# Attention, soft mixture of experts and a wide layer on one core: the small passes of the first token group put in another order

## The chip, the core and the metric

The kernel runs on one core of a Trainium2 chip. A core has five engines that run at the same time and wait for each other by semaphores: TensorE (PE: matmuls, with its weight loads as PEld), VectorE (DVE), ScalarE (ACT), GpSimd (POOL) and SyncE (SP), which here only issues transfers. Each engine takes its instructions strictly in the order in which the program gives them. The metric is the device time of one execution in microseconds (us); lower is better.

## The reference, cut to what matters

Attention over 4 x 8 heads (576 positions, window of 32 positions) gives x of 2304 x 512; a soft mixture of 8 experts turns it into another x of 2304 x 512; the last layer is the one that the change is in:

```python
def _moe2_ref(x, w_in, w_out):            # x 2304x512, w_in 512x2048, w_out 2048x512
    h = x @ w_in
    g = h - np.tanh(h)
    return (g @ w_out).astype(np.float32)
```

The second x is c @ slot_out with c of 2304 x 32, so the kernel never forms it: it forms G = slot_out @ w_in (32 x 2048) and then h = c @ G. The weights w_in and w_out come as 64-bit floats.

## The kernel before, in words

**The last layer's loop** is in `second`. The 2048 hidden units are 16 blocks of 128 (f = 0 to 15), the 2304 tokens four groups of 6, 4, 4 and 4 tiles of 128 tokens. A step is one block for one group. Steps 0 to 7 are the first group (6 tiles, 768 tokens) with blocks 0 to 7; they are what the change is about, and the weights arrive and are prepared while these steps run. Later steps find them ready.

**One step i on TensorE** takes 18 matmuls of 512 columns (line 766): six times w_out's rounded half `whi` with the rounded half `ghi` of g, six times the rest `wlo` with `ghi`, six times `whi` with the rest `glo`. In the middle of the last six stand the two matmuls that make h of step i + 2 (`hidden`, line 735). In steps 0, 1, 2 and 4 there is a projection of w_in to G as well: `project_a` (line 708) between the first six and the next, `project_b` (line 715) after the fourth of the next. `project_a` writes into a free part of the PSUM tile that holds half of h of step i + 1, so it can't start before VectorE has read that half.

**The other engines, for step i + 1, during step i:** ScalarE squares h (line 737), VectorE makes g from it in two pairs of instructions, one pair for 256 columns and one for 512 (`cubic`, lines 744 and 745), ScalarE rounds it (`ghi`, line 751), GpSimd takes the rest (`glo`, line 756).

**Preparing a piece** of the weights (a piece is 128 columns of w_in, called i0 to i15, or 128 rows of w_out, o0 to o15) from its 64-bit form: a short pass makes the low 16 bits (the low pass, line 692 on ScalarE or 694 on GpSimd), a second short pass on GpSimd the top (line 696), and one on VectorE puts them together (`merge`, line 700). A piece of w_out is then rounded by ScalarE into `whi` (line 722), and GpSimd takes the rest `wlo` (line 723); these two are `split_out`. A piece of w_in goes to `project_a`, whose result ScalarE copies twice (lines 710 and 716) and VectorE completes (line 718) before the next `hidden` can use it.

**The order of the work** is written out by hand: the engines' orders follow the order of the calls in the loop over steps and two tables. `now[i]` names the pieces whose top pass (and, earlier, low pass) belongs to step i; `joins[i]` names the pieces merged in step i, first those merged after the rounding of g has been issued, then those merged at the end of the step. Twelve buffers hold 64-bit pieces; a merge frees one, and SyncE then issues the next load.

Of the kernel before, what the change touches and what calls it, by code (L numbers as in the profile page):

```python
# [71 lines left out]
def attention_moe_moe(ctx: ExitStack, tc: tile.TileContext, q, k, v, phi, w1, w2, w_in, w_out, cst, out, dbg=None):  # L72
# [537 lines left out]
    def words(t):  # L610
        r = t.bitcast(I32).rearrange("p (x two) -> p x two", two=2)
        return r[:, :, 1], r[:, :, 0]
# [9 lines left out]
    def second(raw, raws, cT, store):  # L622
# [53 lines left out]
        def drop(piece):  # L676
            raws.pop(piece)
            feed()


        def place(piece):
            kind, f = piece
            return more[:, 512 * (f % 3):512 * (f % 3 + 1)] if kind == "o" and f < NA else flat[:, 512 * (f % 8):512 * (f % 8 + 1)]
# [4 lines left out]
        def prep(piece, on_act=False, parts=(0, 1)):  # L688
            hi, lo = (raws[piece].bitcast(dt).rearrange("p (x four) -> p x four", four=4)[:, :, x] for dt, x in ((I16, 3), (U16, 1)))
            top, low = (place(piece).bitcast(dt).rearrange("p (x two) -> p x two", two=2)[:, :, x] for dt, x in ((BF16, 1), (I16, 0)))  # L690
            if 0 in parts and on_act:
                nc.scalar.activation(out=low, in_=lo, func=AF.Identity, scale=2.0 ** -13, bias=wround)
            elif 0 in parts:
                nc.gpsimd.tensor_scalar(out=low, in0=lo, scalar1=2.0 ** -13, scalar2=WROUND, op0=ALU.mult, op1=ALU.add)
            if 1 in parts:
                nc.gpsimd.tensor_scalar(out=top, in0=hi, scalar1=2.0, scalar2=-2.0, op0=ALU.min, op1=ALU.max)

        def merge(piece, keep=False):
            w = place(piece).bitcast(I32)
            nc.vector.scalar_tensor_tensor(out=w, in0=words(raws[piece])[0], scalar=3, in1=w, op0=ALU.logical_shift_left, op1=ALU.bitwise_xor)  # L700
            if not keep:
                drop(piece)
# [17 lines left out]
        def split_out(f):  # L720
            wf = place(("o", f))
            nc.scalar.copy(whi[:, f, :], wf)
            nc.gpsimd.tensor_tensor(out=wlo[:, f, :], in0=wf, in1=whi[:, f, :].bitcast(F32), op=ALU.subtract)
# [15 lines left out]
        def cubic(i):  # L739
            u, t = us.pop(i), el.tile([128, WMAX], F32, tag="t", name=f"t_{i}")  # L740
            ts[i] = t[:, 0:128 * steps[i][1]]
            for c, hp in hps[i]:
                hp = hp[:, 0:c.stop - c.start]
                nc.vector.scalar_tensor_tensor(out=hp, in0=hp, scalar=-2.0 / 15.0, in1=u[:, c], op0=ALU.mult, op1=ALU.mult)  # L744
                nc.vector.scalar_tensor_tensor(out=t[:, c], in0=u[:, c], scalar=-2.5, in1=hp, op0=ALU.add, op1=ALU.mult)  # L745
# [14 lines left out]
        def outer(i, t, acc, parts=(0, 1, 2)):  # L760
            t0, _, f = steps[i]
            ghi, glo = gg[i]
            whole = t0 == g3[0]
            for x in parts:
                g = (ghi, ghi, glo)[x][:, 128 * t:128 * (t + 1)]
                nc.tensor.matmul(acc, lhsT=g, rhs=(whi, wlo, whi)[x][:, f, :], start=x == 0 and f in ((0,) if whole else (0, NA)), stop=x == 2 and f in ((NF - 1,) if whole else (NA - 1, NF - 1)))  # L766
# [23 lines left out]
        pieces = lambda names: [(x[0], int(x[1:])) for x in names.split()]  # L790
# [2 lines left out]
        again = inner[:NA] + outers  # L793
        todo = pieces("i0 o0 i1 o1 i2 i3 o2 i4 i5 o3 o4 i6 i7 o5 o6 o7") + inner[NA:] + outers[NA:] + again
        now = {i: pieces(x) for i, x in enumerate(("o2 i4", "i5 o3", "o4 i6", "i7 o5", "o6", "o7"))}
        joins = {i: [pieces(y) for y in x] for i, x in enumerate((("i3", "o2"), ("i4", "i5 o3"), ("", "o4"), ("i6", "i7 o5"), ("", "o6"), ("", "o7")))}
        batch = {0: (2, 1), 1: (3, 1), 2: (4, 2), 4: (6, 2)}
        then = {NA + k + k // 2: x for k, x in enumerate(inner[NA:] + outers[NA:])}

# [47 lines left out]
        for i, (t0, n, f) in enumerate(steps):  # L847
            if f == 0 or f == NA and t0 != g3[0]:
                accs = [ps.tile([128, DM], F32, tag=f"acc{t}", name=f"acc{t}_{i}", bufs=1) for t in range(n)]
            first, last = i < NA, f in (NA - 1, NF - 1)  # L850
            if first and not last:
                p = batch.get(i)
                if i:
                    split_out(i + 1)
                for t in range(n):
                    outer(i, t, accs[t], (0,))
                cubic(i + 1)
                if i == 0:
                    split_out(1)
                    for piece in now[0]:  # L860
                        prep(piece, on_act=True, parts=(0,))
                for piece in now.get(i, ()):
                    prep(piece, parts=(1,))
                if p:
                    pj = hps[i + 1][0][1][:, 256:256 + 128 * p[1]]
                    project_a(*p, pj)
                for t in range(n):
                    outer(i, t, accs[t], (1,))
                    if p and t == 3:
                        project_b(*p, pj, (0,))  # L870
                split_g(i + 1, (0,))
                for piece in joins.get(i, ((), ()))[0]:
                    merge(piece)
                if p:
                    project_b(*p, pj, (1,))
                for t in range(n):
                    outer(i, t, accs[t], (2,))
                    if t == 2:
                        hidden(i + 2)
                for piece in now.get(i + 1, ()):  # L880
                    prep(piece, on_act=True, parts=(0,))
                split_g(i + 1, (1,))
                for piece in joins.get(i, ((), ()))[1]:
                    merge(piece)
            else:
                if first:
                    cubic(i + 1)
                if i + 1 < len(steps):
                    split_g(i + 1)
                if i == len(steps) - 2:  # L890
                    for t, j in ((0, 0), (1, 0), (0, 1), (1, 1), (2, 0), (2, 1), (3, 0), (3, 1)):
                        outer(i + j, t, accs[t])
                        if j:
                            finish(i + 1, t, accs[t])
                    break
                for x in (0, 1) if first else ():
                    for t in range(n):
                        outer(i, t, accs[t], (x,))
                if i + 2 < len(steps):
                    hidden(i + 2)  # L900
                    cubic(i + 2)
                for t in range(n):
                    outer(i, t, accs[t], (2,) if first else (0, 1, 2))
                    if last:
                        finish(i, t, accs[t])
                for piece in made:
                    split_out(piece[1])
                made = []
                for piece in ready:
                    merge(piece, keep=piece[0] == "i")  # L910
                    if piece[0] == "i":
                        check.append(piece)
                    else:
                        made.append(piece)
                ready = [then[i]] if i in then else []
                for piece in ready:
                    prep(piece, on_act=True)
                for k, at in enumerate((NA, NA + 4)):
                    at += NA - 2 + 2 * k
                    if i in (at, at + 1):  # L920
                        (project_a, project_b)[i - at](NA + 4 * k, 4, ps.tile([128, 512], F32, tag="acc5", name=f"g{i - at}_{k}", bufs=1))
                if i == NB0:
                    assert not check
                    check = list(again)
                for _ in range(min(len(check), 1)):
                    inspect(check.pop(0))
                if NA <= i < 2 * NA or NB0 <= i < NB0 + NA:
                    nc.vector.tensor_reduce(out=gmx[:, f if i >= NB0 else i - NA:][:, 0:1], in_=Gs[:, 128 * (f if i >= NB0 else i - NA):][:, 0:128].bitcast(F32), axis=AX.X, op=ALU.max, apply_absolute_value=True)
                if i == len(steps) - NA:
                    assert not check and not todo  # L930
                    judge()
                if i == len(steps) - NA + 2:
                    verdict()
            gg.pop(i)
            hps.pop(i, None)
# [167 lines left out]
```

## Time and profile before

| | |
|---|---|
| time, median of 3 runs | 442.32 us (441.25 to 442.57) |
| the profiled execution | 443.09 us, its span 441.3 us |
| TensorE | busy 414.5 us, 94% of the span |
| VectorE | busy 314.8 us, 71% |
| ScalarE | busy 235.2 us, 53% |
| GpSimd | busy 209.5 us, 47% |
| mean granted clock of TensorE | 0.978 of full speed |

The span is the time from the first to the last instruction of that one execution; the time of an execution is 1.8 us longer. A share of busy time is a mean over stages, so it says which engine leads, and not where it waits: for that one goes to the waits of the engine in a stretch and to the order of its instructions in time.

### The profile page before, as it was taken

What the parts mean: (1) busy time and instruction counts of PE and PEld (TensorE: products, weight loads), DVE (VectorE), ACT (ScalarE), POOL (GpSimd) and SP (SyncE); (2) the same over time, 40 slices, a digit from 0 to 9 for tenths busy, and PEclk for the clock granted to TensorE, in tenths of its full rate; (3) what the DMA queues carried; (4) which work ended last, traced back from release to release, by engine and by line L of the source; (5) the groups of instructions that cost most, each with busy time, mean ns of one, the idle gap of its engine ahead of it and who ended that gap; (6) DMA issues with size and microseconds to landing.
All of it is one profiled execution on the core that took longest, in us unless ns stands there. A gap on an engine that the chain in (4) does not pass through costs nothing.

```text
span 441.3 us, 8666 instructions
## 1 busy us (share of the span) xinstructions
PE 414.5 (94%) x3000; PEld 316.9 (72%) x3000; DVE 314.8 (71%) x879; ACT 235.2 (53%) x503; POOL 209.5 (47%) x230
## 2 busy tenths in 40 slices
PE   8989969999998999999779999999999999999994
PEld 5879858878875644356558776777888788888773
DVE  5787856887876362248766678877879987799852
ACT  2565654657854232158645567666775745456430
POOL 1663534543520011069765555458993443434340
PEclk9998987999999999999988999999999999999999
DMA  5698997889897889999751122333445552030202
GB/s 152 168 242 228 222 244 192 228 243 253 254 312 269 335 298 408 401 369 381 250 187 53 42 97 95 97 99 110 128 142 190 195 188 97 0 143 1 95 0 102
DMA packets 59585, 82.84 MB, mean 188 GB/s; under 512 B 22928, under 2 KB 45072, under 8 KB 59536
## 3 DMA queue, kind: packets, MB, share of 16 engines
q1 hardware_dynamic: 59536, 82.23, 58.5%
q8 instruction: 25, 0.41, 0.4%
q14 instruction: 24, 0.20, 0.2%
HBM read 77.50 MB, written 4.72 MB: 186 GB/s over the span
## 4 chain that ended last, share of the span: by engine, by line


## 5 line engine op out<-in xcount | busy, mean ns | idle before, releaser
L756 POOL TENSOR_TENSOR glo<-t,ghi 128x512 fp32r<-128x512 f32 (+2 forms) x63 | 92.5, 1469 | 88.6 <-ACT ghi L751 86.2
L766 PE MATMUL acc<-whi,glo 128*128 128x512 f32 x288 | 108.5, 396 | 0.5 <-POOL glo L756 0.4
L766 PE MATMUL acc<-wlo,ghi 128*128 128x512 f32 x288 | 108.8, 399 | 0.0
L766 PE MATMUL acc<-whi,ghi 128*128 128x512 f32 x288 | 107.5, 395 | 0.2 <-ACT ghi L841 0.2
L751 ACT CAST ghi<-t 128x512 fp32r<-128x512 f32 (+1 forms) x63 | 42.4, 673 | 72.0 <-PE acc L766 33.3
L744 DVE SCALAR_TENSOR_TENSOR h<-h,u 128x512 f32<-128x512 f32 (+1 forms) x78 | 50.2, 644 | 28.9 <-ACT u L737 27.7
L766 PEld LDWEIGHTS acc<-whi,glo 128*128 128x128 f32 x288 | 54.5, 189 | 14.8 <-POOL glo L756 2.4
L766 PEld LDWEIGHTS acc<-wlo,ghi 128*128 128x128 f32 x288 | 54.4, 191 | 13.4 <-issue 1.2
L766 PEld LDWEIGHTS acc<-whi,ghi 128*128 128x128 f32 x288 | 53.9, 188 | 12.7 <-ACT ghi L841 0.8
L745 DVE SCALAR_TENSOR_TENSOR t<-u,h 128x512 f32<-128x512 f32 (+1 forms) x78 | 49.7, 637 | 6.9 <-POOL glo L756 0.5
L737 ACT ACTIVATE u<-h 128x512 f32<-128x512 f32 (+1 forms) x78 | 41.5, 552 | 4.6 <-PE h L735 4.6
L302 ACT COPY pT<-pp 96x512 f32<-96x512 f32 x38 | 22.2, 583 | 34.4 <-PE pp L301 33.9
L283 DVE CUSTOM_DVE_ANT_0 sm<-sc,m_sb 128x96 f32<-128x96 f32 x144 | 29.4, 259 | 14.9 <-PE sc L279 10.7
L279 PE MATMUL sc<-kT,qbd 128*128 128x96 f32 x272 | 39.7, 287 | 0.3 <-DVE kT L210 0.2
L279 PEld LDWEIGHTS sc<-kT,qbd 128*128 128x128 f32 x272 | 35.1, 199 | 2.8 <-issue 1.8
L154 POOL TENSOR_SCALAR km<-k 72x512 f32<-72x512 f32 x30 | 20.4, 695 | 25.7 <-DMA k<-in_k 12.6
L154 POOL TENSOR_SCALAR qm<-q 72x512 f32<-72x512 f32 x30 | 19.1, 652 | 27.7 <-DMA q<-in_q 14.0
L312 PE MATMUL pv<-vw,pT 96*64 96x65 f32 x608 | 26.7, 228 | 3.8 <-POOL vw L177 3.7
L735 PE MATMUL h<-cT,Gs 128*128 128x512 f32 (+1 forms) x78 | 29.0, 398 | 0.3 <-DVE t L745 0.2
L312 PEld LDWEIGHTS pv<-vw,pT 96*64 96x64 f32 x608 | 21.1, 137 | 10.1 <-issue 4.2
L301 PE MATMUL pp<-c_sb,sm 128*96 128x128 f32 x152 | 23.9, 281 | 0.7 <-ACT sm L294 0.7
L287 DVE TENSOR_TENSOR sm<-sm,mx 128x384 f32<-128x384 f32 (+1 forms) x38 | 22.3, 588 | 1.2
(193 smaller groups left out, 674.8 us busy)
## 6 DMA issues: line engine op xcount, KB each, us to landing
w<-in_moe_w SPq DMA_DIRECT2D x60, 512.0 KB
raw_o<-in_moe_w_out SPq DMA_DIRECT2D x32, 512.0 KB
raw_i<-in_moe_w_in SPq DMA_DIRECT2D x22, 512.0 KB
q<-in_q SPq DMA_DIRECT2D x32, 144.0 KB
k<-in_k SPq DMA_DIRECT2D x32, 144.0 KB
out<-X SPq DMA_DIRECT2D x17, 256.0 KB
vw<-in_v SPq DMA_DIRECT2D x16, 144.0 KB
vw<-in_v SPq DMA_DIRECT2D x32, 64.0 KB
```

The lines of the kernel that those rows point to most:

```text
L154: nc.gpsimd.tensor_scalar(out=dst, in0=src, scalar1=1.0, scalar2=0.0, op0=ALU.mult, op1=ALU.add)
L279: nc.tensor.matmul(sc[:, o:o + n, :].rearrange("p g k -> p (g k)"), lhsT=qbd[u % NQ][:, j].rearrange("p a n -> p (a n)"), rhs=keys, start= ...
L283: nc.vector.tensor_tensor_reduce(out=sm[:, o:o + n, :].rearrange("p g k -> p (g k)"), in0=sc[:, o:o + n, :].rearrange("p g k -> p (g k)"), ...
L301: nc.tensor.transpose(pp[:, i, :], sm[:, i, :], ident)
L312: nc.tensor.matmul(pv[64 * ab:64 * ab + 64, i, :], lhsT=pT[:, o + x, 64 * ab:64 * ab + 64], rhs=w[:, ab, u % 2, j + x, :], start=x == 0, s ...
L735: nc.tensor.matmul(hp[:, 0:y - x], lhsT=Gs[:, 128 * f:128 * (f + 1)], rhs=cT[:, t0 + x:t0 + y], start=True, stop=True)
L737: nc.scalar.activation(out=us[i][:, c], in_=hp[:, 0:c.stop - c.start], func=AF.Square)
L744: nc.vector.scalar_tensor_tensor(out=hp, in0=hp, scalar=-2.0 / 15.0, in1=u[:, c], op0=ALU.mult, op1=ALU.mult)
L745: nc.vector.scalar_tensor_tensor(out=t[:, c], in0=u[:, c], scalar=-2.5, in1=hp, op0=ALU.add, op1=ALU.mult)
L751: nc.scalar.copy(gg[i][0], ts[i])
L756: nc.gpsimd.tensor_tensor(out=glo[:, 0:p], in0=t[:, 0:p], in1=ghi[:, 0:p].bitcast(F32), op=ALU.subtract)
L766: nc.tensor.matmul(acc, lhsT=g, rhs=(whi, wlo, whi)[x][:, f, :], start=x == 0 and f in ((0,) if whole else (0, NA)), stop=x == 2 and f in ...
```

## The change

In the first group's steps the merges of the pieces move. Before, most of them stand at a step's end, ahead of the next step's `cubic` on VectorE; now they stand in the middle of the next step, behind its `cubic`. The rounding of the next piece of w_out (`split_out`) moves from a step's beginning to the place behind that merge. The low passes of w_out's pieces move by a step, and the low passes of i5 and i7 go from ScalarE to GpSimd, where the short passes of a step now stand ahead of that step's rounding rest.

```diff
-        joins = {i: [pieces(y) for y in x] for i, x in enumerate((("i3", "o2"), ("i4", "i5 o3"), ("", "o4"), ("i6", "i7 o5"), ("", "o6"), ("", "o7")))}
+        joins = {i: [pieces(y) for y in x] for i, x in enumerate((("i3", ""), ("o2 i4", "i5"), ("o3", ""), ("o4 i6", "i7"), ("o5", ""), ("o6", ""), ("o7", "")))}
+        both = pieces("i5 i7")
+        aside = {i: pieces(x) for i, x in enumerate(("o2 i4", "o3", "o4 i6", "o5", "o6", "o7"))}
...
-                if i:
-                    split_out(i + 1)
                 for t in range(n):
                     outer(i, t, accs[t], (0,))
                 cubic(i + 1)
                 if i == 0:
                     split_out(1)
-                    for piece in now[0]:
-                        prep(piece, on_act=True, parts=(0,))
                 for piece in now.get(i, ()):
-                    prep(piece, parts=(1,))
+                    prep(piece, parts=(0, 1) if piece in both else (1,))
...
                 for piece in joins.get(i, ((), ()))[0]:
                     merge(piece)
+                if i:
+                    split_out(i + 1)
                 if p:
                     project_b(*p, pj, (1,))
...
-                for piece in now.get(i + 1, ()):
+                for piece in aside.get(i, ()):
                     prep(piece, on_act=True, parts=(0,))
```

On VectorE, from the merge of i4 in step 1 on. Here `raw_i_48`, `raw_i_47`, `raw_o_46`, `raw_o_45`, `raw_i_44`, `raw_i_43`, `raw_o_42` are the 64-bit forms of i4, i5, o3, o4, i6, i7, o5 (the number counts the loads still to come), and L744 and L745 are the `cubic` of step 3. Before:

```order
L700 SCALAR_TENSOR_TENSOR X_79<-raw_i_48_2846,X_79 128x512
L718 TENSOR_TENSOR Gs<-h_2_3082,Gs 64x128
L700 SCALAR_TENSOR_TENSOR X_79<-raw_i_47_2848,X_79 128x512
L700 SCALAR_TENSOR_TENSOR more<-raw_o_46_2850,more 128x512
L744 SCALAR_TENSOR_TENSOR h_3_3137<-h_3_3137,u_3136 128x256
L745 SCALAR_TENSOR_TENSOR t_3163<-u_3136,h_3_3137 128x256
L744 SCALAR_TENSOR_TENSOR h_3139<-h_3139,u_3136 128x512
L745 SCALAR_TENSOR_TENSOR t_3163<-u_3136,h_3139 128x512
L718 TENSOR_TENSOR Gs<-h_3_3137,Gs 64x256
```

and now:

```order
L700 SCALAR_TENSOR_TENSOR X_79<-raw_i_48_2846,X_79 128x512
L718 TENSOR_TENSOR Gs<-h_2_3080,Gs 64x128
L700 SCALAR_TENSOR_TENSOR X_79<-raw_i_47_2848,X_79 128x512
L744 SCALAR_TENSOR_TENSOR h_3_3136<-h_3_3136,u_3135 128x256
L745 SCALAR_TENSOR_TENSOR t_3156<-u_3135,h_3_3136 128x256
L744 SCALAR_TENSOR_TENSOR h_3138<-h_3138,u_3135 128x512
L745 SCALAR_TENSOR_TENSOR t_3156<-u_3135,h_3138 128x512
L700 SCALAR_TENSOR_TENSOR more<-raw_o_46_2850,more 128x512
L718 TENSOR_TENSOR Gs<-h_3_3136,Gs 64x256
```

The merge of o3 has gone behind the `cubic` of step 3; i5's stays ahead of it.

On VectorE again, from step 3's `cubic` (which makes g of step 4) to that of step 4. Before:

```order
L744 SCALAR_TENSOR_TENSOR h_3194<-h_3194,u_3191 128x512
L745 SCALAR_TENSOR_TENSOR t_3215<-u_3191,h_3194 128x512
L700 SCALAR_TENSOR_TENSOR X_79<-raw_i_44_2854,X_79 128x512
L700 SCALAR_TENSOR_TENSOR X_79<-raw_i_43_2893,X_79 128x512
L700 SCALAR_TENSOR_TENSOR more<-raw_o_42_2898,more 128x512
L744 SCALAR_TENSOR_TENSOR h_5_3238<-h_5_3238,u_3237 128x256
L745 SCALAR_TENSOR_TENSOR t_3263<-u_3237,h_5_3238 128x256
```

and now:

```order
L744 SCALAR_TENSOR_TENSOR h_3192<-h_3192,u_3189 128x512
L745 SCALAR_TENSOR_TENSOR t_3208<-u_3189,h_3192 128x512
L700 SCALAR_TENSOR_TENSOR more<-raw_o_45_2852,more 128x512
L700 SCALAR_TENSOR_TENSOR X_79<-raw_i_44_2854,X_79 128x512
L700 SCALAR_TENSOR_TENSOR X_79<-raw_i_43_2893,X_79 128x512
L744 SCALAR_TENSOR_TENSOR h_5_3237<-h_5_3237,u_3236 128x256
L745 SCALAR_TENSOR_TENSOR t_3257<-u_3236,h_5_3237 128x256
```

There are three merges between the two in either order; o5's has left the place, o4's has come to it.

On GpSimd, from the rest `glo` of step 3 to that of step 4, before:

```order
L756 TENSOR_TENSOR glo_3185<-t_3163,ghi_3184 128x768
L723 TENSOR_TENSOR wlo<-more,whi 128x512
L696 TENSOR_SCALAR X_79<-raw_i_43_2893 128x512
L696 TENSOR_SCALAR more<-raw_o_42_2898 128x512
L756 TENSOR_TENSOR glo_3229<-t_3215,ghi_3228 128x768
```

and now:

```order
L756 TENSOR_TENSOR glo_3178<-t_3156,ghi_3177 128x768
L694 TENSOR_SCALAR X_79<-raw_i_43_2893 128x512
L696 TENSOR_SCALAR X_79<-raw_i_43_2893 128x512
L696 TENSOR_SCALAR more<-raw_o_42_2898 128x512
L723 TENSOR_TENSOR wlo<-more,whi 128x512
L756 TENSOR_TENSOR glo_3223<-t_3208,ghi_3222 128x768
```

i7's low pass (line 694) is new here, and w_out's rest (line 723) stands behind the short passes, next to `glo`.

## Rows read from the trace of the kernel before

**Rows 1.** The page, part 1: busy time, share of the span, instructions.

```profile
PE 414.5 (94%) x3000; PEld 316.9 (72%) x3000; DVE 314.8 (71%) x879; ACT 235.2 (53%) x503; POOL 209.5 (47%) x230
```

**Rows 2.** Waits, 199 to 249.2 us: who waited for whom: us, times, longest.

```profile
PE h L708 <- DVE t L745: 5.2, 2, 2.8
```

**Rows 3.** Waits of TensorE, 245 to 441 us.

```profile
PE acc L766 <- POOL glo L756: 0.4, 1, 0.4
PE h L735 <- DVE t L745: 0.2, 1, 0.2
```

**Rows 4.** TensorE in time: start, us, instruction, count, [idle before, releaser].

```profile
211.47 1.55 PE L766 MATMUL acc<-whi,ghi 128*128 128x512 f32 x6
215.45 0.64 PE L708 MATMUL h<-X,soT 128*32 128x256 f32 x8 [2.42 <-DVE t L745]
...
218.64 0.56 PE L735 MATMUL h<-cT,Gs 128*128 128x256 f32 x2
...
219.73 1.55 PE L766 MATMUL acc<-whi,ghi 128*128 128x512 f32 x6
221.12 1.53 PE L766 MATMUL acc<-wlo,ghi 128*128 128x512 f32 x6
...
224.20 1.53 PE L766 MATMUL acc<-whi,ghi 128*128 128x512 f32 x6
228.50 1.08 PE L708 MATMUL h<-X,soT 128*32 128x256 f32 x8 [2.77 <-DVE t L745]
...
235.49 1.53 PE L766 MATMUL acc<-whi,ghi 128*128 128x512 f32 x6
...
239.94 1.53 PE L766 MATMUL acc<-whi,ghi 128*128 128x512 f32 x6
```

**Rows 5.** Stretches: length, busy PE, PEld, DVE, ACT, POOL, granted clock, DMA share, GB/s.

```profile
224.20:228.50 4.30, 1.53 (x7) 0.96 (x6) 4.27 (x5) 1.54 (x3) 3.02 (x3) 0.91 0.68 226
...
230.00:232.00 2.00, 2.00 (x7) 1.53 (x6) 0.00 (x0) 0.01 (x1) 0.31 (x1) 0.50 0.09 37
```

**Rows 6.** VectorE in time, columns as in rows 4.

```profile
210.99 1.15 DVE L700 SCALAR_TENSOR_TENSOR X<-raw_i,X 128x512 int32<-128x512 int32 x1 [0.93 <-POOL X L696]
212.07 2.32 DVE L700 SCALAR_TENSOR_TENSOR more<-raw_o,more 128x512 int32<-128x512 int32 x1
214.42 0.43 DVE L744 SCALAR_TENSOR_TENSOR h<-h,u 128x256 f32<-128x256 f32 x1
...
215.95 0.69 DVE L745 SCALAR_TENSOR_TENSOR t<-u,h 128x512 f32<-128x512 f32 x1
...
225.26 2.30 DVE L700 SCALAR_TENSOR_TENSOR more<-raw_o,more 128x512 int32<-128x512 int32 x1
227.49 0.42 DVE L744 SCALAR_TENSOR_TENSOR h<-h,u 128x256 f32<-128x256 f32 x1
```

**Rows 7.** GpSimd in time, columns as in rows 4.

```profile
205.65 2.27 POOL L756 TENSOR_TENSOR glo<-t,ghi 128x768 fp32r<-128x768 f32 x1
...
211.59 2.24 POOL L756 TENSOR_TENSOR glo<-t,ghi 128x768 fp32r<-128x768 f32 x1
215.17 1.30 POOL L723 TENSOR_TENSOR wlo<-more,whi 128x512 fp32r<-128x512 f32 x1 [1.33 <-ACT whi L722]
...
224.08 0.78 POOL L696 TENSOR_SCALAR more<-raw_o 128x512 bf16<-128x512 int16 x1
224.79 2.22 POOL L756 TENSOR_TENSOR glo<-t,ghi 128x768 fp32r<-128x768 f32 x1
...
238.91 1.84 POOL L756 TENSOR_TENSOR glo<-t,ghi 128x768 fp32r<-128x768 f32 x1
```

**Rows 8.** ScalarE in time, columns as in rows 4.

```profile
217.95 0.84 ACT L751 CAST ghi<-t 128x768 fp32r<-128x768 f32 x1
219.00 0.87 ACT L737 ACTIVATE u<-h 128x256 f32<-128x256 f32 x2 [0.21 <-PE h L735]
...
221.22 0.62 ACT L722 CAST whi<-more 128x512 fp32r<-128x512 f32 x1
```

## The prediction, as it was put on record

> **What bounds the kernel now.** I read the page's busy shares first: TensorE leads with 94% [rows 1], so a microsecond is only won where TensorE waits or runs slow. Then its waits. From 245 us on it waits 0.6 us in all until the end [rows 3], so nothing is to be had there and whatever is won before goes through to the end. In the first group one pair stands out: `project_a` (line 708) waits twice for VectorE's `cubic` (line 745), 5.2 us together [rows 2]. TensorE's rows in time show where: at 215.45 in step 2 and at 228.50 in step 4 [rows 4].
>
> What each costs comes from the steps themselves. Steps 2 and 4 have the same instructions. Six matmuls are issued in 1.39 us (219.73 to 221.12), and from `project_a` to the next step's first matmul step 2 takes 4.28 us (215.45 to 219.73), so the step without a wait is 5.67 us [rows 4]. Step 2 took 8.26 us (211.47 to 219.73): 2.59 us too long, all of it the gap. Step 4 took 11.29 us (224.20 to 235.49): 5.62 us too long [rows 4], of which 2.91 us are the gap (228.50 less 224.20 and 1.39) and 2.71 us a slower clock: the same work after `project_a` took 6.99 us and not 4.28. Around this gap the granted clock fell to 0.91 of full speed on average and then stood at 0.50, the lower level of 1.2 GHz [rows 5]; after the gap of step 2 it did not fall, since the same work there needed no more than 4.28 us. Together 8.21 us.
>
> Why `cubic` is late is seen by laying VectorE's rows beside GpSimd's. The merge of o3 takes 2.32 us, from 212.07 to 214.39, while GpSimd's `glo` runs to 213.83; in step 4 o5's takes 2.30 us, to 227.56, with `glo` to 227.01 [rows 6, 7]. Both end 0.56 us behind GpSimd's end, so a merge waits until the GpSimd instruction beside it is over and then needs 0.56 us. `cubic`, queued behind it, starts at 214.42 and 227.49, and its first pair is what `project_a` waits for [rows 6]. A merge gets its turn between two GpSimd instructions: i5's ran 1.15 us to 212.14, and `glo`, next in GpSimd's order from 211.59, was stretched to 2.24 us where it takes 1.84 otherwise [rows 6, 7].
>
> **The change part by part.** TensorE's instructions and order stay as they are, and so do VectorE's count and the loads' order. I lay the steps out by hand with these durations: merge 0.56 us behind GpSimd's end; short pass 0.71 us back to back (224.08 to 224.79), `wlo` 1.30, `glo` 1.84 [rows 7]; first pair of `cubic` 0.85 us (two of 0.43), all four 2.22 us (214.42 to 216.64) [rows 6]; `ghi` 0.84, both squares 0.87, the first after 0.4, `whi` 0.62 [rows 8]; `hidden` 3.19 us behind `project_a` (218.64) [rows 4].
>
> *Step 2.* The merge of o3 leaves the place ahead of `cubic`. i5's stays. On GpSimd three short passes now follow the `glo` of step 1, which ended at 207.92 stretched [rows 7] and should end near 207.6: with a turn for the merges of o2 and i4 between them they end near 210.85 (207.6 + 3 x 0.71 + 2 x 0.56), and i5's merge near 211.4. ScalarE's first square is there by then too (`hidden` stands 1.09 us ahead of a step's first matmul, 218.64 to 219.73 [rows 4], so at 210.4), and `cubic` runs from 211.45. Its first pair is done at 212.3, and TensorE wants it at 212.86 (211.47 + 1.39). The gap of 2.59 us goes; step 3 starts near 217.1 instead of 219.73.
>
> *What is late next, step 4.* `wlo` of o2 now goes ahead of `glo` on GpSimd: 211.4 to 212.7, then `glo` to 214.5. The merge of o3, behind `cubic` (to 213.7), waits for that and ends at 215.05. `whi` of o3, now behind `ghi` of step 3 on ScalarE, ends at 216.75; the squares for step 4 queue behind it, so that `cubic` in step 3 runs from 217.2 to 219.4. On GpSimd `wlo` goes from 216.8 to 218.1 and `glo` to 219.95. Now merges and short passes take turns: merge o4 to 220.5, i7's low pass to 221.2, merge i6 to 221.75, i7's top pass to 222.45, o5's pass to 223.15, merge i7 to 223.7. Only then does step 4's `cubic` start; its first pair ends at 224.55 and `project_a` starts at 224.65. Step 4 begins at 217.13 plus 4.47 (step 3 has no wait: 219.73 to 224.20 [rows 4]), 221.6, and wants `project_a` at 223.0. So a gap of 1.65 us stays of the 2.91. Is it long enough for the clock? The gap of 2.59 us in step 2 was not [rows 4], so I take the full clock and win the 2.71 us too.
>
> *Costs put at little.* The low passes of i5 and i7 add two GpSimd instructions, 1.4 us; they are in the chain above, and i5's runs ahead of step 2 beside TensorE's step 1. On ScalarE the low passes only move to idle time. Loads: by this hand schedule the passes of i4, i5, o3 and i6 come later than before, so their loads have more time; the next group wants its pieces 6 us sooner, but SyncE issues those loads on the merges, which shift with the steps. `whi` on ScalarE is due at a step's start: o3's at 216.75 for 217.1, o4's at 221.2 for 221.6, so it holds, with 0.4 us to spare. `glo` is due after twelve matmuls, 2.8 us into a step without projection: 219.95 against 219.9 in step 3. From there a loop runs through the steps: end of `glo`, merge 0.56, `whi` 0.62, `wlo` 1.30, `glo` 1.84, and three hand-overs of some 0.05: 4.47 us. A step of TensorE is 4.45 us (235.49 to 239.94 [rows 4]). The two are equal, so `glo` comes just in time or a little late in steps 3, 5 and 6; I take 0.3 us for all of them, between 0 and 1.5 (0.3 in each of five steps).
>
> **The sum.** 8.21 less 1.65 less 0.3 is 6.3 us won. Against the profiled execution's 443.09 us this is 436.8; the median of the runs lies 0.77 us lower, so 442.32 becomes 436.0 us. Ends of the unknowns: if merges and passes meet less often (the chain without o5's pass and one wait, 1.3 us) almost no gap stays in step 4, 434.4, and no more than 8.21 can be won, 434.1. If the `glo` loop takes its 1.5, 437.2.
>
> The rule that speaks most against this change is in the Trainium skill, SBUF — State Buffer, section Who interferes with whom: VectorE with two inputs in SBUF and GpSimd exclude each other for the whole instruction, and the order of issue decides who waits. The trace agrees as far as [rows 6, 7] show it, and they add that the turn changes after each instruction. Read without that turn, the merges of o2 and i4 in step 1 would wait for two short passes more, 1.4 us; the instruction behind them (line 718) holds up `hidden`, step 2 would start that much later, and the sum would come to 437.4.
>
> **The rivals.**
>
> *A, the clock falls all the same.* The gap that stays in step 4 is followed by the slow level as before: 2.71 us more, 438.7. For it: the clock did fall at this place, behind a gap only 0.3 us longer than that of step 2. Against it: the gap of 2.59 us in step 2 left the clock as it was, and 1.65 us is well below it. It would take some 1 us more in the chain to step 4.
>
> *B, GpSimd becomes the bound.* The loop of 4.47 us has one short pass in the way in each of steps 3 to 7, 0.78 us each: five times that, 3.9 us, gives 439.9. For it: the loop has no slack, and the page's 47% of GpSimd hides that it is nearly full in these steps. Against it: the short pass stands where GpSimd waits for `whi` anyway (merge, hand-over and `whi` take 1.2 us, the pass behind the merge 1.3).
>
> *C, slower.* The same loop, but each merge meets a whole `glo` more: 1.84 us, 6.3 us a step against 4.45. Over steps 3 to 7 that is 9.2 us and eats the 8.21, so 443.3, and 446.0 with one fall of the clock. It decides from a loop of 6.1 us on. Against it: the merge stands directly behind one `glo`, and the next `glo` needs that merge's own `whi` through `wlo`'s place in the order, so a merge can't meet two.
>
> *D, nothing stays.* The time is given back in the later groups, because GpSimd or a load is late there: 442.3. Against it: TensorE waits 0.6 us there in all [rows 3], and those steps depend on this group's end only through TensorE's own order.
>
> **How the numbers follow.** The forecast (434.1 to 437.4) has 0.68, A 0.14, B 0.08, D 0.06, C 0.04. The range of 434.0 to 439.2 holds the forecast and most of A. A measurement of this kernel can tell 0.3%, 1.3 us, from no change. Forecast, A and B are faster by more than that, 0.90; D is the same, 0.06; C slower, 0.04.
>
> **What would show it.** Right: `project_a` in step 2 without a wait; in step 4 a gap of 1 to 2 us behind `cubic`; no stretch at 0.50 of the clock after 200 us; merges of w_out's pieces of 0.7 to 1.2 us behind `cubic`, each ending 0.56 us behind a `glo`; step 6 starting near 233.6 instead of 239.94. Wrong: TensorE waiting for `glo` or `whi` in each of steps 3 to 7 (B, C), a stretch at half clock (A), or new waits behind 243 us (D).

## The result, and the profile after

The changed kernel takes 436.83 us (median of 4 runs, 436.69 to 437.73) against 442.44 us of the kernel before beside it (4 runs, 441.25 to 444.16): a ratio of 0.9874 with an interval of 0.9839 to 0.991. Forecast were 436.0 us and a range of 434.0 to 439.2. Ratios and intervals, here and below, are taken over the faster executions alone, so they need not be the quotient of the medians beside them. The profiled execution took 436.85 us with a span of 435.1 us, where the one of before had 443.09 and 441.3.

The page's first part after the change:

```profile
PE 412.4 (95%) x3000; PEld 315.1 (72%) x3000; DVE 314.3 (72%) x879; ACT 233.8 (54%) x501; POOL 210.9 (48%) x232
```

The busy shares hardly moved [rows 1]; the waits did. First those of TensorE from 199 to 245 us, then those from 240 to 436 us (the pair, us in all, times, longest):

```profile
PE h L708 <- DVE t L745: 1.0, 1, 1.0
...
PE acc L766 <- POOL glo L756: 0.4, 1, 0.4
PE acc L766 <- ACT ghi L751: 0.2, 1, 0.2
PE h L735 <- DVE t L745: 0.2, 1, 0.2
```

`project_a` waits once and for 1.0 us where it waited twice and for 5.2 [rows 2], and behind the group TensorE waits 0.8 us in all where it waited 0.6 [rows 3]. TensorE in time after the change:

```profile
200.02 1.35 PE L766 MATMUL acc<-whi,ghi 128*128 128x512 f32 x4
...
211.62 1.55 PE L766 MATMUL acc<-whi,ghi 128*128 128x512 f32 x6
213.11 0.64 PE L708 MATMUL h<-X,soT 128*32 128x256 f32 x8
...
217.40 1.54 PE L766 MATMUL acc<-whi,ghi 128*128 128x512 f32 x6
...
220.24 0.96 PE L766 MATMUL acc<-whi,glo 128*128 128x512 f32 x3
...
222.09 1.55 PE L766 MATMUL acc<-whi,ghi 128*128 128x512 f32 x6
224.63 0.64 PE L708 MATMUL h<-X,soT 128*32 128x256 f32 x8 [1.00 <-DVE t L745]
...
228.91 1.55 PE L766 MATMUL acc<-whi,ghi 128*128 128x512 f32 x6
...
233.58 1.52 PE L766 MATMUL acc<-whi,ghi 128*128 128x512 f32 x6
...
242.53 0.39 PE L766 MATMUL acc<-whi,ghi 128*128 128x512 f32 x1
```

What the whole group took is read from the first matmul of step 0 to that of step 8. Before, these two stood at:

```profile
199.89 1.34 PE L766 MATMUL acc<-whi,ghi 128*128 128x512 f32 x4
...
249.12 0.39 PE L766 MATMUL acc<-whi,ghi 128*128 128x512 f32 x1
```

The start of a step is read off its first row of `whi` with `ghi`. Step 2 takes 5.78 us (211.62 to 217.40) instead of 8.26, step 4 takes 6.82 (222.09 to 228.91) instead of 11.29 [rows 4]. Steps 3 and 5 take 4.69 and 4.67, some 0.2 more than before: the three matmuls that first need `glo` start 2.84 us into step 3 (220.24) instead of 2.75, and take 0.96 us instead of 0.84. From step 0 to step 8 the group takes 42.51 us (it starts at 200.02) instead of 49.23 (199.89 to 249.12): 6.72 us less. Of these the span kept 6.2. The same stretches as in [rows 5]:

```profile
224.20:228.50 4.30, 3.87 (x23) 2.84 (x24) 3.37 (x5) 2.01 (x5) 3.62 (x3) 1.00 0.74 244
230.00:232.00 2.00, 2.00 (x9) 1.41 (x9) 1.97 (x3) 0.86 (x2) 2.00 (x2) 1.00 0.00 0
```

The granted clock is 1.00 in both, the upper level of 2.4 GHz. VectorE in time after the change:

```profile
211.31 0.43 DVE L744 SCALAR_TENSOR_TENSOR h<-h,u 128x256 f32<-128x256 f32 x1
...
213.45 1.27 DVE L700 SCALAR_TENSOR_TENSOR more<-raw_o,more 128x512 int32<-128x512 int32 x1
...
219.51 1.23 DVE L700 SCALAR_TENSOR_TENSOR more<-raw_o,more 128x512 int32<-128x512 int32 x1
220.65 1.20 DVE L700 SCALAR_TENSOR_TENSOR X<-raw_i,X 128x512 int32<-128x512 int32 x1
222.53 1.16 DVE L700 SCALAR_TENSOR_TENSOR X<-raw_i,X 128x512 int32<-128x512 int32 x1 [0.68 <-POOL X L696]
223.61 0.42 DVE L744 SCALAR_TENSOR_TENSOR h<-h,u 128x256 f32<-128x256 f32 x1
```

and GpSimd:

```profile
212.34 1.83 POOL L756 TENSOR_TENSOR glo<-t,ghi 128x768 fp32r<-128x768 f32 x1
...
218.31 1.87 POOL L756 TENSOR_TENSOR glo<-t,ghi 128x768 fp32r<-128x768 f32 x1
220.27 1.11 POOL L694 TENSOR_SCALAR X<-raw_i 128x512 int16<-128x512 uint16 x1
221.44 1.05 POOL L696 TENSOR_SCALAR X<-raw_i 128x512 bf16<-128x512 int16 x1
222.43 0.78 POOL L696 TENSOR_SCALAR more<-raw_o 128x512 bf16<-128x512 int16 x1
223.14 1.69 POOL L723 TENSOR_TENSOR wlo<-more,whi 128x512 fp32r<-128x512 f32 x1
```

Step 2's `cubic` starts at 211.31, 0.31 us ahead of the step; before it was 2.95 us behind the step's start. The merges of o3 and o4 end at 214.72 and 220.74, 0.55 and 0.56 us behind a `glo` (214.17 and 220.18); they take 1.27 and 1.23 us, a little more than the 0.7 to 1.2 that the prediction gave as a sign. In step 3 one sees the turns: merge of o4, i7's low pass (stretched to 1.11 us), merge of i6, i7's top pass (1.05), o5's pass, merge of i7, then `cubic` at 223.61. Between the merge of i6 and that of i7 VectorE is idle for 0.68 us, since i7's top pass isn't done.

### The profile page after: what moved, and what is told of

Its sections match the earlier page's. It is cut to its first block, busy times and chain, and to the rows that moved or that the text cites. A ratio compares the mean times of both kernels' runs of the same rounds, so it can differ in the third digit from the quotient of the medians.

```text
span 435.1 us, 8667 instructions
## 1 busy us (share of the span) xinstructions
PE 412.4 (95%) x3000; PEld 315.1 (72%) x3000; DVE 314.3 (72%) x879; ACT 233.8 (54%) x501; POOL 210.9 (48%) x232
## 4 chain that ended last, share of the span: by engine, by line
## 5 line engine op out<-in xcount | busy, mean ns | idle before, releaser
L756 POOL TENSOR_TENSOR glo<-t,ghi 128x512 fp32r<-128x512 f32 (+2 forms) x63 | 91.0, 1445 | 82.8 <-ACT ghi L751 79.0
L766 PE MATMUL acc<-wlo,ghi 128*128 128x512 f32 x288 | 107.4, 393 | 0.0
L744 DVE SCALAR_TENSOR_TENSOR h<-h,u 128x512 f32<-128x512 f32 (+1 forms) x78 | 50.3, 645 | 32.3 <-ACT u L737 31.1
L745 DVE SCALAR_TENSOR_TENSOR t<-u,h 128x512 f32<-128x512 f32 (+1 forms) x78 | 49.7, 637 | 7.6 <-POOL glo L756 0.5
L154 POOL TENSOR_SCALAR km<-k 72x512 f32<-72x512 f32 x30 | 19.4, 661 | 26.2 <-PE pp L301 8.4
L287 DVE TENSOR_TENSOR sm<-sm,mx 128x384 f32<-128x384 f32 (+1 forms) x38 | 23.8, 626 | 1.2
```

Of the source, the lines that this page charges most:

```text
L154: nc.gpsimd.tensor_scalar(out=dst, in0=src, scalar1=1.0, scalar2=0.0, op0=ALU.mult, op1=ALU.add)
L756: nc.gpsimd.tensor_tensor(out=glo[:, 0:p], in0=t[:, 0:p], in1=ghi[:, 0:p].bitcast(F32), op=ALU.subtract)
```

## The experiments

A gap below is, as in the prediction, the start of `project_a` less the step's start and 1.39 us; "behind it" is the time from `project_a` to the next step's first matmul, 4.28 us at the full clock. The halves, the halved `glo` and the low passes on ScalarE ran on one chip, where the kernel before took 443.32 us (25 runs, 439.59 to 448.28); the filled gaps, o5's pass, the change once more and the last version ran on another, where it took 442.55 (28 runs, 437.52 to 446.58). Three more profiles of the kernel before come from a third chip. Each experiment has one profile.

### One half of the change at a time

The early half has steps 0 to 2 as in the change and the rest as before, the late half the steps from 3 on. The edits against the change, early half:

```diff
-joins = ... ("o3", ""), ("o4 i6", "i7"), ("o5", ""), ("o6", ""), ("o7", "")
+joins = ... ("o3", "o4"), ("i6", "i7 o5"), ("", "o6"), ("", "o7")
...
-                if i:
+                if 0 < i < 3:
                     split_out(i + 1)
```

and late half:

```diff
-joins = ("i3", ""), ("o2 i4", "i5"), ("o3", ""), ("o4 i6", "i7"), ...
+joins = ("i3", "o2"), ("i4", "i5 o3"), ("", ""), ("o4 i6", "i7"), ...
...
-                if i:
+                if i > 2:
                     split_out(i + 1)
```

(The low passes go with their pieces, and `split_out` stands at the step's beginning in the other steps.)

> The change for steps 0 to 2 alone; from step 3 on the merges and the rounding of w_out stand as before (i6, i7 and o5 merged ahead of step 4's cubic). If the two gaps are separate terms, step 2 has no wait for cubic and step 4 keeps a gap of 2.5 to 3.3 us. Theory 1, one gap of that length is enough for the lower clock: the stretch at 0.50 stays, about 2.6 us are won, 439.8 us. Theory 2, the clock fell only because step 2's gap came before it: no stretch at 0.50, 5.3 us won, 437.1 us. Rival, the merges' place does not matter: step 2 waits as before, 442.4 us.

> The change from step 3 on alone; in steps 0 to 2 the merges and the rounding of w_out stand as before. Step 2 keeps its gap of 2.6 us, step 4's falls to 1.0 to 1.5 us and the clock stays full: 1.7 and 2.7 us won, about 438.0 us. If the clock falls even after a short gap: 440.7 us. Rival, the place does not matter: 442.4 us.

The early half: 440.89 us (10 runs, 435.69 to 443.27), a ratio of 0.9967 with an interval of 0.9929 to 1.0004. The late half: 438.49 us (10 runs, 436.4 to 442.4), 0.991 with 0.9867 to 0.9953. TensorE in step 4 of the early half:

```profile
219.91 1.55 PE L766 MATMUL acc<-whi,ghi 128*128 128x512 f32 x6
224.81 0.64 PE L708 MATMUL h<-X,soT 128*32 128x256 f32 x8 [3.35 <-DVE t L745]
229.10 1.54 PE L766 MATMUL acc<-whi,ghi 128*128 128x512 f32 x6
```

and in steps 2 and 4 of the late half:

```profile
216.22 0.64 PE L708 MATMUL h<-X,soT 128*32 128x256 f32 x8 [2.45 <-DVE t L745]
222.06 1.54 PE L766 MATMUL acc<-whi,ghi 128*128 128x512 f32 x6
...
228.72 0.64 PE L708 MATMUL h<-X,soT 128*32 128x256 f32 x8 [0.66 <-DVE t L745]
```

Each half takes away the gap of its own step and leaves the other: the early half has 0.09 us in step 2 and 3.51 in step 4, the late half 2.61 in step 2 and 0.80 in step 4. So the two gaps have separate causes, as the prediction had them. Their lengths aren't wholly independent: 3.51 lies above the 2.5 to 3.3 that were expected and 0.80 below the 1.0 to 1.5. This fits a TensorE that comes sooner to step 4, and waits longer there, where step 2 has no gap; it was not tested by itself. The medians lie above the values expected as well, by 1.1 us over theory 1's 439.8 and by 0.5 over 438.0. On the clock the prediction is contradicted. Behind 3.35 us of waiting the same work took 4.29 us: no fall. Behind the 2.45 us in step 2 it took 5.84: a fall, in the place where the profile of before had none. The early half's profile is that of its fastest execution (435.69 us), 5.2 us below the median, so it shows that a fall can stay out and not how often.

### The rest `glo` in two halves, in the kernel before

Rows of VectorE and GpSimd alone can't tell whether a merge waits for the one GpSimd instruction beside it or for a stretch of GpSimd's work. Cutting `glo` tells it: the work stays, the instruction gets shorter.

```diff
-nc.gpsimd.tensor_tensor(out=glo[:, 0:p], in0=t[:, 0:p], in1=ghi[:, 0:p].bitcast(F32), op=ALU.subtract)
+for x, y in ((0, p // 2), (p // 2, p)) if i in (2, 4) else ((0, p),):
+    nc.gpsimd.tensor_tensor(out=glo[:, x:y], in0=t[:, x:y], in1=ghi[:, x:y].bitcast(F32), op=ALU.subtract)
```

> The kernel before, with GpSimd's rest glo for steps 2 and 4 taken in two instructions of 384 columns instead of one of 768; VectorE's order is that of before. Turn theory (a merge waits for the one GpSimd instruction beside it and then needs 0.56 us): the merges of o3 and o5 fall from 2.3 to about 1.5 us although GpSimd has more to do (2.2 us instead of 1.84), cubic starts 0.7 to 0.8 us earlier in steps 2 and 4, both gaps shrink by as much, 440.9 us with the lower clock as before, 438.2 us if it stays full after a gap of 2.1 us. Rival, the two engines share bandwidth or the merge waits until GpSimd's work on that step is done: the merges stay at 2.3 us or grow to 2.6, 442.4 to 443 us.

439.39 us (10 runs, 438.48 to 443.06), 0.9934 with 0.9899 to 0.9968: between the 440.9 expected with the lower clock and the 438.2 without. The merge of o3 on VectorE and the two halves on GpSimd:

```profile
212.09 1.51 DVE L700 SCALAR_TENSOR_TENSOR more<-raw_o,more 128x512 int32<-128x512 int32 x1
...
211.62 2.84 POOL L757 TENSOR_TENSOR glo<-t,ghi 128x384 fp32r<-128x384 f32 x2
```

GpSimd takes longer over the two (2.84 us) than it took over the one (2.24), and yet the merge ends sooner: 1.51 us instead of 2.32 [rows 6, 7], 1.49 instead of 2.30 for o5's. Both gaps shrink by 0.8 us, to 1.81 and 2.11. So the merge waits for one instruction and takes the next turn. On the clock: behind the gap of 1.81 us the work took 4.27 us, behind that of 2.11 us 5.83, so here the clock fell behind a gap shorter than the 2.59 us that left it alone before.

### One pass less in the row ahead of step 4's cubic, and one more

First the change with the low passes of i5 and i7 back on ScalarE:

```diff
-both = pieces("i5 i7")
-aside = ... ("o2 i4", "o3", "o4 i6", "o5", "o6", "o7")
+both = []
+aside = ... ("o2 i4 i5", "o3", "o4 i6 i7", "o5", "o6", "o7")
```

> The changed kernel, with the low passes of i5 and i7 on ScalarE again (behind the other low passes of steps 0 and 2), so GpSimd has one short pass less in steps 1 and 3. Turn theory: one pass of 0.71 us and one turn less stand ahead of i7's merge, but the merge of i6 takes the pass's place and o5's pass comes ahead of i7's merge, so cubic of step 4 starts only some 0.4 us earlier, the gap there is 0.6 to 0.9 instead of 1.15 us, and step 1 loses its 0.2 us before hidden: 436.2 us against 436.8. If GpSimd's load alone set the gap: it goes altogether, 435.5 us. If ScalarE's order matters more (three low passes ahead of the rounding of g): no gain or some 0.3 us lost.

436.49 us (4 runs, 435.71 to 440.76). In its profile `project_a` of step 4 waits 0.34 us:

```profile
223.27 0.64 PE L708 MATMUL h<-X,soT 128*32 128x256 f32 x8 [0.34 <-DVE t L745]
```

The gap is 0.47 us where the change had 1.15: less than the 0.6 to 0.9 that the turns were to leave, but not gone, as it should be if GpSimd's load alone set it. The group takes 41.68 us, 0.83 less than with the change; 0.68 of it is this gap, and 0.10 lies in step 1, where i5's low pass was. So the new low passes on GpSimd weren't free: the prediction had i7's in its chain, and 0.68 us is its price.

Then the change with o5's short pass moved from step 3 to step 2, so that GpSimd has less to do ahead of step 4's `cubic`, but `wlo` (1.30 us) behind i7's top pass instead of a short pass:

```diff
-now = ... "o4 i6", "i7 o5", "o6", "o7"
+now = ... "o4 i6 o5", "i7", "o6", "o7"
```

> The change with one GpSimd instruction moved: o5's short pass goes from step 3 to step 2, so that behind i7's top pass GpSimd has w_out's rest (1.30 us alone, 1.69 beside a merge) next in its order instead of a short pass (0.78 us). Theory (turns: i7's merge becomes ready as i7's top pass ends, the next GpSimd instruction is issued at the same time and goes first, so the merge ends some 0.56 us behind that instruction): GpSimd does less ahead of step 4's cubic, and yet cubic comes later, by 0.4 to 0.7 us; the gap in step 4 is 1.5 to 1.9 us where the change had 1.15, and step 0 to step 8 takes 42.8 to 43.3 us; median 437 to 437.6. Rival (what counts is GpSimd's amount of work ahead of that merge): the gap falls by 0.7 us to about 0.4 and the median to about 436.

437.73 us (10 runs, 435.46 to 439.61), 0.9907 with 0.9873 to 0.994. VectorE, GpSimd and TensorE at the place:

```profile
221.74 1.75 DVE L700 SCALAR_TENSOR_TENSOR X<-raw_i,X 128x512 int32<-128x512 int32 x1 [0.68 <-POOL X L696]
223.41 0.42 DVE L744 SCALAR_TENSOR_TENSOR h<-h,u 128x256 f32<-128x256 f32 x1
...
221.63 1.31 POOL L723 TENSOR_TENSOR wlo<-more,whi 128x512 fp32r<-128x512 f32 x1
...
224.43 0.64 PE L708 MATMUL h<-X,soT 128*32 128x256 f32 x8 [1.62 <-DVE t L745]
```

The merge of i7 becomes ready as the top pass ends; `wlo` starts 0.11 us ahead of it and goes first, and the merge ends 0.55 us behind `wlo` (223.49 and 222.94). Less work on GpSimd made `cubic` later: the gap is 1.76 us, the group 43.07, both inside what the theory of turns gave and outside the rival's 0.4 us. The median is 0.1 us above what was expected, and medians of ten runs don't separate this kernel from the change (437.73 and 437.86 on the same chip); what is said here rests on the rows of one profile.

### The clock: the kernel before with its gaps filled, and its profile three times more

Eleven more matmuls with weights of zero, which add nothing to the sum, stand in the gaps of steps 2 and 4:

```diff
+if i in (2, 4):
+    for _ in range(11):
+        nc.tensor.matmul(accs[5], lhsT=zero, rhs=whi[:, f, :], start=False, stop=False)
 project_a(*p, pj)
```

> The kernel before with eleven more matmuls of 512 columns in step 2 and eleven in step 4, between the first six and project_a, where TensorE waits: their weights are zeros and they add nothing to the sum; 11 x 0.23 us fill 2.5 us of each gap. Theory (the clock falls because TensorE stood idle there, and only in some executions): project_a starts when it did, the clock stays at 1.00 through steps 4 and 5, step 0 to step 8 takes about 46.5 us (49.2 less 2.7), and all executions fall in one group at 439.5 to 440.5 where the kernel before has two, at 442 to 444 and at 439.5 to 440.2. Rival (the slower clock has nothing to do with the gap): the times are spread as those of the kernel before and the median stays within 0.5 us of it. Third (the added matmuls end behind the time at which project_a could start): up to 0.3 us more in each step.

441.01 us (12 runs, 438.9 to 447.04), 0.997 with 0.9941 to 0.9998. TensorE in steps 2 and 4:

```profile
218.29 0.64 PE L708 MATMUL h<-X,soT 128*32 128x256 f32 x8
...
231.37 0.64 PE L708 MATMUL h<-X,soT 128*32 128x256 f32 x8 [0.34 <-DVE t L745]
235.65 1.54 PE L766 MATMUL acc<-whi,ghi 128*128 128x512 f32 x6
```

`project_a` starts where it did (2.58 us behind the six matmuls in step 2, 2.97 in step 4), and behind it the work takes 4.27 and 4.28 us: no fall. The group takes 46.82 us, 2.41 less than in the first profile of before, with the gaps still there in length. By the medians the filling is worth 1.5 us (interval 0.1 to 2.6). Each execution's mean granted clock is on record too: its median is 0.9875 over the 12 filled ones, 0.982 over the 28 of the kernel before and 0.986 over 11 of the change on the same chip. All this fits a fall that comes from TensorE standing idle in the gap. But the profile is one, and a gap without a fall is seen in the kernel before as well, so it isn't proved. Two things were missed: the median lies above the 439.5 to 440.5 expected, and the runs do not fall into one narrow group. Their spread of several us has another source; the next runs show one place where it arises.

Is the fall there in each execution? Three profiles more of the kernel before, unchanged:

> The kernel before once more, for its profile alone. Theory (the gaps of steps 2 and 4 are the same in every execution, the fall of the clock behind them is not): a gap of 2.4 to 2.6 us in step 2 and of 2.7 to 3.1 in step 4 again; from project_a to the next step's first matmul either 4.28 us (clock kept) or 6.9 to 7.0 (clock fallen), and over three such profiles not always the same place. Rival (the longer gap always makes the clock fall, the shorter never): 4.28 us in step 2 and 6.99 in step 4 in each of the three.

> As the run before it: the gaps again 2.4 to 2.6 and 2.7 to 3.1 us; theory: 4.28 or about 7.0 us behind each, not always in the same place; rival: 4.28 behind step 2's and 6.99 behind step 4's each time.

> As the two runs before it. Theory and rival as there; of the three profiles the theory expects at least one with another pattern than 4.28 and 6.99 us.

They took 447.8, 443.76 and 444.31 us. `project_a` and the next step's start, steps 2 and 4, in the first:

```profile
219.06 0.73 PE L708 MATMUL h<-X,soT 128*32 128x256 f32 x8 [2.44 <-DVE t L745]
224.85 1.53 PE L766 MATMUL acc<-whi,ghi 128*128 128x512 f32 x6
...
233.64 1.08 PE L708 MATMUL h<-X,soT 128*32 128x256 f32 x8 [2.80 <-DVE t L745]
240.75 1.52 PE L766 MATMUL acc<-whi,ghi 128*128 128x512 f32 x6
```

and in the second:

```profile
217.70 1.08 PE L708 MATMUL h<-X,soT 128*32 128x256 f32 x8 [2.43 <-DVE t L745]
223.50 1.53 PE L766 MATMUL acc<-whi,ghi 128*128 128x512 f32 x6
...
232.28 0.64 PE L708 MATMUL h<-X,soT 128*32 128x256 f32 x8 [2.80 <-DVE t L745]
236.55 1.54 PE L766 MATMUL acc<-whi,ghi 128*128 128x512 f32 x6
```

Four profiles of one kernel, with gaps alike to 0.05 us:

| profile | behind step 2's gap, over 4.28 | behind step 4's, over 4.28 | group | group less both |
|---|---|---|---|---|
| first (on record ahead of the prediction) | 0 | 2.71 | 49.23 | 46.52 |
| second | 1.51 | 2.83 | 50.89 | 46.55 |
| third | 1.52 | 0 | 48.07 | 46.55 |
| fourth | 1.55 | 1.53 | 49.60 | 46.52 |

The theory holds in its main point and the rival falls: which gap the clock falls behind, and whether it costs 1.5 or 2.8 us, differs from execution to execution; everything else in the group is the same to 0.03 us. That the three on one chip already differ shows that it is not the chip alone. A price of 1.5 us, 5.8 us for the work behind a gap, was in neither the theory's list nor the rival's. The group also starts at 199.89, 203.47, 202.12 and 200.88 us in the four, though the program ahead of it is one and the same. The stretch from 80 to 120 us, in the second profile and in the fourth, shows one place where they part:

```profile
80.00:120.00 40.00, 37.42 (x443) 32.54 (x440) 29.65 (x150) 23.79 (x69) 21.76 (x38) 0.91 0.88 237
```

```profile
80.00:120.00 40.00, 37.96 (x489) 33.28 (x484) 32.82 (x166) 27.15 (x75) 21.51 (x38) 1.00 0.84 231
```

The clock stood at 0.91 on average in the one and at 1.00 in the other, and fewer matmuls were done. This is not all of it: the first and the fourth profile have the same granted clock, to two digits, in each stretch of 40 us up to 200, and still start the group 0.99 us apart.

### The change once more, and a version that beats it

> The changed kernel itself once more, beside the kernel before on the same chip, to see how each one's times are spread. Theory (the two gaps are certain in every execution; the fall of the clock behind them comes only in some executions of the kernel before, and costs 2.7 us there): the changed kernel, whose only gap is about 1.15 us in step 4, keeps the full clock and shows one narrow group of times, 436.0 to 437.5; the kernel before shows two groups, most executions at 442 to 444 and some at 439.5 to 440.2; the medians differ by 5.5 to 6.5 us. Rival (the clock falls in every execution of the kernel before, and the spread has another cause): the changed kernel shows the same two groups, about 2.7 us apart, at 434 and 437. Third: the clock may fall behind a gap of 1.15 us too: then a part of the executions at 439 to 440.

437.86 us (11 runs, 436.29 to 440.26) against 442.55: 0.99 with 0.9867 to 0.9932. The profile repeats the first one: `project_a` in step 4 waits 1.01 us, behind it 4.27 us, the group takes 42.56 us. Neither the narrow group of times nor the full difference came (4.7 us by the medians where 5.5 to 6.5 were expected): what differs between executions lies ahead of the group too. The third case, a fall behind the gap of 1.15 us, is in neither profile of the change.

What stays of the gap is the row of turns ahead of step 4's `cubic`. So i6 is merged in step 2, where VectorE is idle behind line 718, and both low passes stay on ScalarE:

```diff
-joins: ... ("o3", ""), ("o4 i6", "i7"), ...
+joins: ... ("o3", "i6"), ("o4", "i7"), ...
-both = pieces("i5 i7")
-aside = ... ("o2 i4", "o3", "o4 i6", "o5", "o6", "o7")
+both = []
+aside = ... ("o2 i4 i5", "o3 i6", "o4 i7", "o5", "o6", "o7")
```

> The change with i6's merge at the end of step 2 instead of the middle of step 4's preparation, i7's at the end of step 3 without i7's low pass on GpSimd (both low passes, i5's and i7's, on ScalarE). Theory (what remains of the wait in step 4 is the row of merges and short passes that take turns ahead of its cubic: merge o4, i7's low pass, merge i6, i7's top pass, o5's pass, merge i7): with one merge and one pass less in that row, 0.56 to 0.7 us each, cubic of step 4 starts about 1.2 us earlier, the gap in step 4 falls from 1.15 to 0 to 0.3 us, and step 0 to step 8 takes 41.1 to 41.6 us where the change took 42.51; the median 435.2 to 435.9. Rival (cubic of step 4 waits for the squares on ScalarE, that stand behind w_out's rounding, rather than for the merges): the gap stays above 0.8 us and the time at 436.5.

435.35 us (6 runs, 434.21 to 436.67), 0.9851 with 0.9806 to 0.9896, beside the change's 437.86 on the same chip, a difference of 2.5 us. i6's merge on VectorE, and TensorE in step 4:

```profile
215.14 0.69 DVE L700 SCALAR_TENSOR_TENSOR X<-raw_i,X 128x512 int32<-128x512 int32 x1
...
220.98 1.52 PE L766 MATMUL acc<-whi,ghi 128*128 128x512 f32 x6
222.43 0.64 PE L708 MATMUL h<-X,soT 128*32 128x256 f32 x8
```

The merge meets no GpSimd instruction and takes 0.69 us, and `project_a` no longer waits. The group takes 41.30 us, 1.21 less than with the change, as expected; 0.83 of this the low passes on ScalarE had given without the early merge. The rest of the medians' 2.5 us isn't in the group's rows and stays unexplained. Steps 3 and 5 still take 4.66 and 4.68 us: the loop through `glo` is what is left.

## Why the prediction was right, point by point

**The mechanism held.** `cubic` was late since a merge ahead of it waited for a whole `glo`. With o3's merge moved, step 2 has no wait; with o5's moved, step 4 has less. The turns were shown twice from outside: a shorter `glo` shortens the merge by its own 0.8 us, and a longer instruction in the turn lengthens it. In the second of these `wlo` started 0.11 us earlier and went first. `cubic`, one of whose inputs is in PSUM, takes 0.42 us at 223.61 beside `wlo`, as ever. The Trainium skill (SBUF — State Buffer, section Who interferes with whom) states that the order of issue decides who blocks; the 0.11 us agree. The Trainium skill states in the same section that a VectorE instruction with at most one input in SBUF, outside the modes that use two ports, doesn't contend with GpSimd; the 0.42 us agree. The case that was priced without the turn, 437.4 us, did not come: line 718 held up no step by 1.4 us, step 1 took 5.45 us (206.17 to 211.62) and 5.27 before.

**The terms of the sum**, forecast and measured, in us of the group:

| term | forecast | measured |
|---|---|---|
| gap of step 2 | 2.59 | 2.48 (8.26 less 5.78) |
| gap of step 4 | 2.91 less 1.65 | 2.91 less 1.15 |
| slower clock behind step 4's gap | 2.71 | 2.71 between these two profiles |
| `glo` late, and the rest | -0.3 | -0.23 (two steps by +0.22, one +0.18, two by -0.16 and -0.23) |
| sum | 6.3 | 6.72 |

The gap that stays was mis-sized for a reason that the hand schedule shows: `cubic` of step 4 was forecast for 223.7 and came at 223.61, `project_a` for 224.65 and came at 224.63. TensorE, forecast for 221.6 at the step's start, came at 222.09. So the 0.5 us are no gain: 0.13 of them are the group's own later start, and the rest lies in steps 1 to 3. Step 6 was forecast for 233.6 and started at 233.58. Two slips of the prediction are without effect: 1.3 us off the chain would give 434.7 and not 434.4, and executions of the kernel before spread over 9 us on one chip, so that a few of them can't tell 0.3%.

**The step that failed** is the clock, though its figure came out. The prediction said that a gap of 2.59 us "was not" long enough, and took the fall behind 2.91 us for a fixed price. The four profiles show 0, 1.5 or 2.8 us behind either gap. The mean of their sums, (2.71 + 4.34 + 1.52 + 3.08) / 4 = 2.91, is near the forecast's 2.71 by luck: too much was put on one gap and nothing on the other. With the halved `glo` the clock fell behind a gap of 2.11 us, so that 1.65 us is "well below" 2.59 was a weak reason against rival A, though A did not come. What the gaps cost in every execution is 46.53 less 42.53, 4.0 us (forecast 3.55: 2.59 + 1.26 - 0.3); the clock's fall cost 1.5 to 4.3 us on top in the four that were seen.

**The rivals.** A did not come: none of the six profiles with the change in step 4, with gaps up to 1.76 us, shows a fall. B and C did not: steps 3 and 5 lost 0.2 us each to `glo`, not 0.78, and step 6 took 4.35. D did not: from step 8 to the span's end it is 192.57 and 192.12 us with the change, and 191.64 to 192.18 in four profiles of before; by the means of these some 0.5 us were given back, about as much as the four differ among themselves.

**What stays open.** The profiles give 6.7 us for the group by the first pair and 6.9 by the means of four and two; the medians give 5.6 us in the result (interval 4.0 to 7.1) and 4.7 where the change ran once more (3.0 to 5.9). Some 0.5 us go in the part behind the group. For the rest, the starts of the group differ by 3.6 us among four executions of one program, and how often the clock falls may differ between chips; neither was shown to be the reason.

## What to carry to other kernels

Lay the rows of VectorE and GpSimd side by side before moving anything: where the two alternate, the instruction that holds the turn ahead of the critical one counts by its own length, and the amount of work behind it does not. Put the longest GpSimd instruction where no VectorE instruction of two SBUF inputs stands ahead of urgent work, and a merge into a stretch where GpSimd is idle. Price a slower clock behind a gap as a spread, from several profiles of the same kernel, never from one.

## What was not expected of the hardware

The clock falls behind like gaps in some executions and not in others. Of eleven waits of 1.97 to 3.35 us ahead of `project_a` in the profiles of the kernel before, of its halves and of the halved `glo`, eight were followed by 1.5 to 2.8 us of slower work and three were not, the longest (3.35 us) among these; of the six waits of 0.34 to 1.65 us, in these profiles and those of the changed kernels, none was. The rows give the counts, and no rule follows from them.
